# Spectral mixing and expert lookup in one pass: the spectral branch from split half precision to float32, its 16-point stages in 32-row blocks, and a new order of the work

## The chip, the cores and the metric

The kernel runs on one core of a Trainium2 chip. A core has a matrix engine (PE, with its weight loads shown apart as PEld), a vector engine (DVE), a scalar engine (ACT), a general engine (POOL) and a queue for transfers (SP); they share an on-chip memory (SBUF) and a smaller one of eight banks in which PE's results land (PSUM). The metric is the device time of one execution, the median of the runs.

## The reference

For a matrix x of 2048 tokens by 576 features the result is x plus two branches on its normalized rows. The first is a filter in frequency space; the second picks one of 64 experts for each of 32 heads.

```python
def _A_ref(x, w_r, w_i):                       # spectral branch
    X = jnp.fft.rfft2(x, axes=(-2, -1))
    X = X * (w_r + 1j * w_i)
    return jnp.fft.irfft2(X, s=(S, D), axes=(-2, -1))

def _B_ref(x, w_q, k1, k2, u, v):              # one of 8 x 8 experts per head
    q = jnp.einsum("nd,dhc->nhc", xf, w_q)
    s1 = jnp.einsum("nhd,ed->nhe", q[..., :dk], k1)
    s2 = jnp.einsum("nhd,ed->nhe", q[..., dk:], k2)
    ...                                        # the best of each, e = 8 * i1 + i2; softmax over one is 1
    act = _gelu(jnp.einsum("nd,nhkd->nhk", xf, u[top_e]))
    return jnp.einsum("nhk,nhk,nhkd->nd", g, act, v[top_e])

xn = _layernorm(x, axis=-1)
return x + _A_ref(xn, w_r, w_i) + _B_ref(xn, w_q, k1, k2, u, v)
```

## The kernel before

The 2048-point transform over tokens is split into 128 x 16. Tokens lie in 16 tiles of 128 rows. In what follows a tile t or group g is one of 16.

**Front.** `ln` normalizes each tile. `folds` (L713) forms even and odd parts of a row in two steps: sum and difference of 289 elements (POOL, tile `t` in the trace), then sums of 145 (POOL and DVE) and a difference of 2 x 144 (DVE), into a tile shown as `A`. ACT makes `Rs`, the scaled matrix of the 128-point transform, and replicates the 33 middle columns three times (`yl`). `dft128` (L731) multiplies on PE and puts the result into two arrays that hold all tiles, `AB` (four parts of 128 rows) and `ABL` (the left-over 33 rows): ACT copies a half-precision high half, DVE subtracts it from the result for the low half.

**Keys.** 32 transfers bring the weights `wq` of the second branch, and `fold_part` multiplies them with the differences of the keys (`KP`), four column tiles of 32 side by side.

**Spectral middle, per group.** `d_fwd` (L981) does the transform over features: one matmul for the left-over rows and six for each half, since every product of two split numbers is three products (high by high, high by low, low by high). Its result is split again into a tile `A`. `s_fwd` (L998) is the 16-point stage over pairs of groups, in blocks of 64 x 64 (`s` against `A`). `s_mul` (L1021) multiplies by the filter `Wt`, divided by a scale `wx` that `load_w` (L796) and `w_scale` (L806) find from the largest value of the filter: two products on DVE into `t`, two sums on POOL into `y`, a high half on ACT and a low half on POOL into `yh`, and a replication on ACT into `yl`. `s_inv` (L1043) is the 16-point stage back, in two row tiles of 64, with `yh` and `yl` as what is held in PE and `s` as what is moved. Its result is split into `AB` and `ABL` again.

**Second branch, in the same stretch.** `x_t` (L889) loads and splits the transposed rows, `scores` (L904) multiplies them with `MU`, `route` (L930) and `combine` (L950) find the chosen expert and its weight on DVE.

**Last stage, per tile.** `d_inv` (L1076) does the transform over features back, with an eviction by ACT (`yh<-banks,sc`), a product with the scale on DVE, a difference and two sums on POOL. `fin` (L1105) multiplies with `RT`, adds the experts' part, adds x on DVE and stores.

**What sets the order.** All operations are first collected, and then issued in an order set by the table `RANK` and by a model of when each operand is ready (`forward`, L404). `LIMIT` (L205) bounds how many tiles of each kind PSUM holds at a time. So every instruction has the line L528 in the trace, that of the call in `issue`; which step it belongs to is read from the names of its operands. In order listings a number behind a name tells buffers apart.

## Time and profile before

| | us |
|---|---|
| median of 3 runs (lowest, highest) | 226.85 (226.66, 227.8) |
| profiled execution, span | 226.4 |
| PE busy (share of the span) | 198.3 (88%) |
| PEld busy | 136.1 (60%) |
| DVE busy | 195.3 (86%) |
| ACT busy | 135.2 (60%) |
| POOL busy | 150.8 (67%) |
| transfers | 43.43 MB, mean 192 GB/s |

Busy times are sums over the one profiled execution; a matmul counts from its start to its modelled end, so matmuls in a row overlap in it, and how much PE can do is better read from the distance between starts. A row of groups reads: line, engine, operation, out<-in, partitions x elements, count, then busy time, mean of one in ns, then the idle time of the engine just ahead of them and what ended it. A float32 matmul is shown as two records. The chain that ended last is 48% PE and 34% DVE.

### The profile page before, as it was taken

To read this page: it belongs to the slowest core of one execution; us is meant where nothing else is said; L and a number is where in the kernel's file an instruction comes from. 1 tells how busy PE (TensorE), PEld (TensorE's weight loads), DVE (VectorE), ACT (ScalarE), POOL (GpSimd) and SP (SyncE) were. 2 spreads that over 40 slices of the span, in tenths; PEclk is the share of its full clock that TensorE was granted. 3 is DMA by queue.
4 is the path that set the end of the run, shared out by engine and by line. 5 is a ranking of instruction groups with operands and counts; after the bars stand their busy time and mean duration, and the time that the engine had idled before them with its cause. 6 is when DMAs were issued, how large, how long until landed. Compare 5 with 4: busy or idle time off the path is not lost.

```text
span 226.4 us, 5987 instructions
## 1 busy us (share of the span) xinstructions
PE 198.3 (88%) x2287; PEld 136.1 (60%) x2287; DVE 195.3 (86%) x423; ACT 135.2 (60%) x294; POOL 150.8 (67%) x217
## 2 busy tenths in 40 slices
PE   0197959999997999899888999999899999999984
PEld 0185536877675367584464665645566767788762
DVE  1979899997769789763999999999999999999843
ACT  2388877888397797949577577545483332242420
POOL 3889887842097829418668585459794977586880
PEclk9999999999999699999999999999999999999999
DMA  6999999979999995533334322200200002223234
GB/s 209 413 430 410 406 409 408 409 254 380 377 385 402 321 356 141 174 99 107 100 114 153 94 80 61 69 4 0 62 3 0 0 3 104 106 110 154 104 115 148
DMA packets 14572, 43.43 MB, mean 192 GB/s; under 512 B 1872, under 2 KB 4688, under 8 KB 14160
## 3 DMA queue, kind: packets, MB, share of 16 engines
q1 hardware_dynamic: 14544, 43.05, 52.0%
q8 instruction: 18, 0.29, 0.6%
q14 instruction: 10, 0.08, 0.1%
HBM read 38.33 MB, written 4.72 MB: 190 GB/s over the span
## 4 chain that ended last, share of the span: by engine, by line
PE 48%; DVE 34%; issue 7%; POOL 4%; ACT 4%; DMA 2%; DVEq 0%; ACTq 0%; POOLq 0%
PE banks L528 48%; DVE MT L528 8%; DVE w L528 6%; DVE t L528 6%; DVE XN L528 3%; POOL t L528 2%; DVE mx L528 2%; DVE A L528 2%; DVE AB L528 2%; DMA XN<-in_x_dram 2%; DVE st L528 1%; POOL A L528 1%; DVE ABL L528 1%; DVE rr L528 1%; ACT yh L528 1%
## 5 line engine op out<-in xcount | busy, mean ns | idle before, releaser
L528 PE MATMUL banks<-MU,xT 128*128 128x512 f16 x192 | 47.5, 379 | 1.1 <-DVE t L528 0.9
L528 POOL TENSOR_TENSOR xT<-xf,xT 128x512 f16<-128x512 f32 (+1 forms) x32 | 26.2, 819 | 16.6 <-ACT xT L528 14.2
L528 POOL TENSOR_TENSOR y<-t,t 128x289 f32<-128x289 f32 x32 | 22.6, 727 | 20.6 <-DVE t L528 20.3
L528 PE MATMUL banks<-c,AB 128*128 128x145 f16 (+1 forms) x384 | 35.2, 227 | 0.0
L528 POOL TENSOR_TENSOR A<-t 128x145 f32<-128x145 f32 (+2 forms) x48 | 31.2, 665 | 5.3 <-DVE t L528 3.1
L528 PEld LDWEIGHTS <-AB 128*128 128x128 f16 x384 | 32.2, 121 | 3.5 <-issue 1.4
L528 PEld LDWEIGHTS <-xT 128*128 128x128 f16 x224 | 20.6, 99 | 22.2 <-issue 2.1
L528 POOL TENSOR_TENSOR t<-XN 128x289 f32<-128x289 f32 x32 | 24.0, 770 | 8.8 <-DVE A L528 4.1
L528 ACT ACTIVATE yh<-banks,sc 128x580 f32<-128x580 f32 x16 | 11.9, 744 | 23.8 <-PE banks L528 16.9
L528 POOL TENSOR_TENSOR yh<-y,yh 128x578 f16<-128x578 f32 x16 | 21.9, 1377 | 5.4 <-ACT yh L528 4.5
L528 DVE SCALAR_TENSOR_TENSOR t<-banks,wx,Wt 128x578 f32<-128x578 f32 x32 | 24.1, 807 | 0.5 <-PE banks L528 0.4
L528 PE MATMUL banks<-A,c 128*128 128x288 f32 x64 | 21.8, 422 | 1.5 <-POOL A L528 0.9
L528 PE MATMUL banks<-Rs,yl 128*99 128x128 f32 x64 | 11.2, 305 | 13.5 <-ACT Rs L528 13.4
L528 PE MATMUL banks<-w,KP 128*32 128x288 f32 x256 | 22.0, 441 | 0.8 <-DVE mm__94 L528 0.8
L528 DVE TENSOR_TENSOR AB<-banks,AB 128x512 f16<-128x512 f32 x32 | 21.4, 675 | 1.3 <-ACT AB L528 0.7
L528 PE MATMUL banks<-c,ABL 99*128 99x289 f16 (+1 forms) x64 | 18.6, 291 | 1.4 <-DVE t L528 1.0
L528 ACT ACTIVATE AB<-banks 128x512 f16<-128x512 f32 x32 | 18.6, 587 | 2.0 <-PE banks L528 1.9
L528 PE MATMUL banks<-Rs,A 128*128 128x128 f32 x128 | 19.0, 298 | 0.0
L528 PEld LDWEIGHTS banks<-Rs,A 128*128 128x128 f32 x128 | 17.1, 209 | 2.5 <-issue 1.4
L528 PEld LDWEIGHTS banks<-Rs,yl 128*99 128x99 f32 x64 | 8.3, 180 | 16.6 <-ACT Rs L528 15.5
L528 DVE TENSOR_REDUCE MT<-w 128x128 bf16<-128x896 bf16 (+1 forms) x16 | 18.1, 1139 | 0.0
L528 ACT ACTIVATE ABL<-banks 99x256 f16<-99x256 f32 x32 | 12.0, 379 | 9.7 <-PE banks L528 9.6
(124 smaller groups left out, 433.3 us busy)
## 6 DMA issues: line engine op xcount, KB each, us to landing
w<-in_wq_dram SPq DMA_DIRECT2D x32, 576.0 KB, 7.0
xf<-in_xT_dram SPq DMA_DIRECT2D x16, 320.0 KB, 3.7
Wt<-in_W_dram SPq DMA_DIRECT2D x8, 578.0 KB, 6.1
out_dram<-XN SPq DMA_DIRECT2D x14, 288.0 KB, 2.1
XN<-in_x_dram SPq DMA_DIRECT2D x3, 1154.0 KB, 10.6
s<-in_s_dram SPq DMA_DIRECT2D x16, 192.0 KB, 3.4
XN<-in_x_dram SPq DMA_DIRECT2D x2, 577.0 KB, 4.6
c<-in_c_dram SPq DMA_DIRECT2D x1, 868.5 KB, 9.8
```

The costliest lines, as they stand in the source:

```text
L528: fn(*[x.place() if isinstance(x, _Ps) else x for x in args], **{k: x.place() if isinstance(x, _Ps) else x for k, x in kw.items()})
```

## The change

The filter's scale and all splits of the spectral branch go; `AB`, `ABL` and the constants are float32. Every product of split numbers becomes one float32 matmul, every split eviction one copy. The scale that was left goes into `RT`. `d_fwd` and `d_inv` work on two tiles at once, with the left-over rows in four row tiles of 32 (`ABL`, four accumulators in four banks). `s_fwd` works on four groups at once in 16 blocks of 32 x 32, real and imaginary part one after the other. `s_inv` has four row tiles of 32 (`y` held, `iv` moved, 64 columns). `dft128` puts its left-over rows into four column tiles of 32. In `route` a reduction over seven becomes three maxima in half the width. The transfers of `s16` (3.07 MB) become `fw` and `iv` (1.57 MB). A string `PICK` says for each of some 370 simple operations which engine does it (v DVE, a ACT, g POOL), and `RANK` is new. Lines that longer functions lose stand in the kernel above.

```diff
@@ -18,12 +18,6 @@
...
-    s16 = np.concatenate(_hl(fw * 64) + _hl(iv), 2)
...
+    fw = fw.reshape(4, 4, 128, 96).transpose(0, 2, 1, 3).astype(np.float32)
+    iv = iv.reshape(8, 2, 128, 96).transpose(0, 2, 1, 3).astype(np.float32)
...
+PICK = (
+    "vgvgagvvvvaavggvgaavggvvaagggvaavgvvvaaavgvgvaavgvvavavvvgvavvggvvaavggvvvavvvvaavgvvvavagvvvgavgggv"
...
 RANK = (
-    2, 13, 11, 15, 48, 86, 12, 14, 6, 4, 3, 5, 1, 53, 51, 54, 58, 7, 0, 8, 10, 9, 18, 21, 24, 20, 16, 23, 29,
...
+    256, 294, 356, 417, 432, 525, 87, 484, 865, 888, 985, 269, 467, 374, 627, 757, 101, 541, 404, 387, 622,
...
-LIMIT = {"x": 2, "a": 4, "b": 4, "c": 4, "s": 2, "f": 1, "m": 2}
+LIMIT = {"x": 2, "a": 4, "b": 4, "q": 8, "c": 4, "s": 2, "f": 1, "m": 2}
...
+class _Flex:
...
+    def _of(self, calls):
...
+        c = PICK[n] if n < len(PICK) else self.pick
+        eng, m, args, kw = calls[c]
+        getattr(plan.of[c], m)(*args, **kw)
...
+    def tt(self, out, a, b, op):
...
+    def copy(self, out, x, scale=None):
...
-    AB = K([128, 2, 4, S], F16, "AB")
-    ABL = K([128, 2, S], F16, "ABL")
+    AB = K([128, 4, S], F32, "AB")
+    ABL = K([128, S], F32, "ABL")
...
     def folds(t):
         xn = XN[:, t]
...
+        e = T([128, 2, L], F32, "eo", 4, "t1")
+        FG.tt(e[:, 1], xn[:, 0:289], xn[:, 576:287:-1], OP.subtract)
+        FV.tt(e[:, 0], xn[:, 0:289], xn[:, 576:287:-1], OP.add)
+        F = T([128, 2, L], F32, "F", 6, "A2")
+        FV.tt(F[:, 1, 0:145], e[:, 1, 0:145], e[:, 1, 288:143:-1], OP.add)
         V.scalar_tensor_tensor(F[:, 0, 0:145], e[:, 0, 0:145], rr[:, 2, t:t + 1], e[:, 0, 288:143:-1],
                                op0=OP.add, op1=OP.add)
...
+        FV.tt(F[:, :, 145:289], e[:, :, 143::-1], e[:, :, 145:289], OP.subtract)
+        Rs = T([128, 128], F32, "Rs", 4, "act")
+        FA.copy(Rs, Rm, rr[:, 0, t:t + 1])
+        FF[t] = (F, Rs)
     @staged
     def dft128(t):
-        F, FL, Rs = FF.pop(t)
+        F, Rs = FF.pop(t)
         p = PS("x")
-        m = p[:, 0].rearrange("p (h e) -> p h e", e=4)
-        l = p[:99, 1, 0:256].rearrange("p (h e) -> p h e", e=4)
+        m = p[:, 0].rearrange("p (h e) -> p h e", e=2)
+        l = p[:, 1, 0:128].rearrange("p (h e) -> p h e", e=2)
         for c in range(4):
             b, s = divmod(c, 2)
             o = 161 if s else 0
             P.matmul(p[:, 0, 128 * c:128 * c + 128], F[:, b, o:o + 128], Rs, start=True, stop=True)
...
+        for c in range(4):
+            b, s = divmod(c, 2)
+            o = 145 if s else 128
+            P.matmul(p[32 * c:32 * c + 32, 1, 0:128], F[:, b, o:o + 32], Rs, start=True, stop=True,
+                     tile_position=(0, 32 * c))
+        FP.copy(AB.rearrange("p c (h n) -> p (c h) n", n=32)[:, :, 2 * t:2 * t + 2], m)
+        FP.copy(ABL.rearrange("p (h n) -> p h n", n=32)[:, :, 2 * t:2 * t + 2], l)
...
+        V.tensor_scalar(RT, RT, sc[:, 10:11], 4.0 / 1179648.0 / 4096.0, op0=OP.mult, op1=OP.mult)
...
-        A.activation(j, w, AF.Abs, accum_out=wm[:, g // 2:g // 2 + 1])
...
-        V.tensor_reduce(v0, wv, axis=AX, op=OP.max)
+        V.tensor_tensor(wv[:, :, 192:384], wv[:, :, 0:192], wv[:, :, 192:384], op=OP.max)
+        V.tensor_tensor(wv[:, :, 320:448], wv[:, :, 192:320], wv[:, :, 320:448], op=OP.max)
+        V.tensor_tensor(v0.rearrange("p (t m) -> p t m", t=2), wv[:, :, 320:384], wv[:, :, 384:448], op=OP.max)
...
     def d_fwd(g):
-        p = PS("a")
+        ps = [PS("a"), PS("a")]
+        plan.pack = {p.tile for p in ps}
+        pv = [p[:, :, 0:290].rearrange("p c (q l) -> p c q l", q=2) for p in ps]
+        for q in range(2):
+            n = slice(128 * (g + q), 128 * (g + q) + 128)
+            for b in range(2):
+                for c in range(2):
+                    P.matmul(pv[b][:, c, q, :], AB[:, 2 * b + (c ^ b), n], dc[:, b, c, :], start=(q == 0), stop=False)
+        for q in range(2):
+            n = slice(128 * (g + q), 128 * (g + q) + 128)
+            for c in range(2):
+                for b in range(2):
+                    i = 2 * b + (c ^ b)
+                    r = slice(32 * i, 32 * i + 17 - i % 2)
+                    P.matmul(pv[b][:, c, q, :], ABL[r, n], dl[r, :], start=False, stop=(q == 1), tile_position=(32 * i, 0))
+        plan.pack = set()
+        t = T([128, 2, 2, 2, 145], F32, "A2", 6)
         for b in range(2):
-            P.matmul(p[:, b, :L], ABLg[:99, b, g, :], dl[:99, b, :], start=True, stop=False)
+            FP.copy(t[:, :, b].rearrange("p q c l -> p c q l"), pv[b])
+        for q in range(2):
+            A2[g + q] = t[:, q].rearrange("p b c l -> p b (c l)")[:, :, :L]
+    PF = {}
+    @staged
+    def s_fwd(g, m):
+        ps = [PS("q", (128, 512)) for q in range(4)]
+        plan.pack, plan.cap = {p.tile for p in ps}, 1000
+        for b in range(2):
+            w = 32 * (0, 1, 1, 2)[2 * m + b]
+            for k in range(4):
+                r = slice(32 * k, 32 * k + 32)
+                for q in range(4):
+                    o = 32 * (k ^ q)
+                    P.matmul(ps[q][o:o + 32, :L], FW[g][r, q, w:w + 32], A2[g + q][r, b, :], start=(b == 0), stop=(b == 1),
+                             tile_position=(32 * k, o))
+        plan.pack, plan.cap = set(), 900
+        for q in range(4):
+            PF[g + q] = ps[q]
+    @staged
+    def s_mul(g, m):
+        x, w = PF.pop(g)[:, :L].unsqueeze(1).to_broadcast([128, 2, L]), Wt[g]
+        if m == 0:
+            Y[g] = T([128, 2, L], F32, "y", 6)
+            V.tensor_tensor(Y[g], x, w, op=OP.mult)
+            return
+        y, t = Y[g], T([128, 2, L], F32, "t1", 4)
+        V.tensor_tensor(t, x, w, op=OP.mult)
+        FG.tt(y[:, 0], y[:, 0], t[:, 1], OP.subtract)
+        FG.tt(y[:, 1], y[:, 1], t[:, 0], OP.add)
+    @staged
+    def s_inv(g):
+        p, s = PS("c", (128, 4, 2, 4, 64)), IV[g]
+        for q in range(NQ):
+            y = Y.pop(g + q)
+            for c in range(3):
+                for ri in range(2):
+                    for k in range(4):
+                        r = slice(32 * k, 32 * k + 32)
+                        o = (0, 161, 49)[c]
+                        P.matmul(p[:, k, q, c, :], y[r, ri, o:o + 128], s[r, q, 32 * ri:32 * ri + 64],
+                                 start=(ri == 0), stop=(ri == 1), tile_position=(32 * k, 0))
+        for q in range(NQ):
+            pq = p[:, :, q]
+            FP.copy(ABg[:, :, g + q, :].rearrange("p c (k n) -> p c k n", k=4),
+                    pq[:, :, 0:2].rearrange("p k c (b n) -> p (c b) k n", b=2))
+            for b in range(2):
+                FP.copy(ABLg[64 * b:64 * b + 64, g + q, :].rearrange("p (k n) -> p k n", k=4),
+                        pq[64:128, :, 2, 32 * b:32 * b + 32])
+    def d_inv(t):
+        ps = [PS("a"), PS("a")]
+        plan.pack = {p.tile for p in ps}
+        pv = [p[:, :, 0:290].rearrange("p c (q l) -> p c q l", q=2) for p in ps]
+        for q in range(2):
+            for b in range(2):
+                for c in range(2):
+                    P.matmul(pv[b][:, c, q, :], ABt[:, 2 * (c ^ b) + b, :, t + q], ic[:, b, c ^ b, :], start=(q == 0), stop=False)
+        for q in range(2):
             for c in range(2):
...
+                for b in range(2):
+                    i = 2 * b + (c ^ b)
+                    r = slice(32 * i, 32 * i + 32)
+                    P.matmul(pv[b][:, c, q, :], ABLt[r, :, t + q], il[r, :], start=False, stop=(q == 1),
+                             tile_position=(32 * i, 0))
         plan.pack = set()
+        es = T([128, 2, 2, 2, 145], F32, "es", 6, "y")
+        eo = T([128, 2, 2, L], F32, "eo2", 4, "t1")
+        y = T([128, 2, D], F32, "yy", 6, "A2")
+        for b in range(2):
+            FP.copy(es[:, b].rearrange("p c q l -> p c (q l)"), ps[b][:, :, 0:290])
+            V.tensor_tensor(eo[:, b, :, 0:145], pv[b][:, 0], es[:, b, 1], op=OP.add)
+            FG.tt(eo[:, b, :, 288:144:-1], es[:, b, 0, :, 0:144], es[:, b, 1, :, 0:144], OP.subtract)
         for q in range(2):
...
+            FG.tt(y[:, q, 0:289], eo[:, 0, q], eo[:, 1, q], OP.add)
+            FG.tt(y[:, q, 575:288:-1], eo[:, 0, q, 1:288], eo[:, 1, q, 1:288], OP.subtract)
         return y
...
-    for r in range(3):
+    for r in range(2):
         x_t(r)
...
+    for g in range(0, 16, 4):
+        for q in (g, g + 2):
+            d_fwd(q)
+            if q > 2:
+                load_w(q)
+            load_iv(q)
+        if g:
+            load_fw(g)
+        for m in range(2):
+            s_fwd(g, m)
+            for q in range(4):
+                s_mul(g + q, m)
+        for q in (g, g + 2):
+            s_inv(q)
+            r = q // 2
+            scores(r)
+            if r < 6:
+                x_t(r + 2)
             route(r)
...
             combine(r)
...
+    y = d_inv(0)
+    for t in range(0, 16, 2):
+        n = d_inv(t + 2) if t < 14 else None
+        for q in range(2):
+            fin(t + q, y[:, q])
+        y = n
...
```

PE, around the first return of the 16-point stage. Before (`c_72` the constants, `yh_136` the split products, `s_0_114` the stage's matrix):

```order
L528 LDWEIGHTS AB
L528 MATMUL banks<-c_72,AB 128x144
L528 LDWEIGHTS AB
L528 MATMUL banks<-c_72,AB 128x145
...
L528 LDWEIGHTS yh_136
L528 MATMUL banks<-s_0_114,yh_136 128x128
```

and now, with the loads of the weights inside the float32 matmuls (`A_93` the evicted columns):

```order
L552 MATMUL banks<-c_72,AB 128x145 x8
L552 MATMUL banks<-c_72,ABL 128x145 x8
L552 MATMUL banks<-w,KP 32x288 x8
L552 MATMUL banks<-A_93,fw 32x289 x32
L552 MATMUL banks<-w,KP 32x288 x4
L552 MATMUL banks<-A_93,fw 32x289 x32
L552 MATMUL banks<-w,KP 32x288 x8
L552 MATMUL banks<-c_72,AB 128x145 x8
L552 MATMUL banks<-c_72,ABL 128x145 x8
L552 MATMUL banks<-w,KP 32x288 x8
L552 MATMUL banks<-iv,y 128x64 x96
```

Four groups go through the forward stage in two sets of 32 blocks, and four come back in one run of 96; groups of the wq fold stand between.

DVE, at the end of the front. Before:

```order
L528 TENSOR_TENSOR AB<-banks,AB 128x128x4
L528 TENSOR_TENSOR ABL<-banks,ABL 33x64x4
L528 TENSOR_TENSOR AB<-banks,AB 128x128x4
L528 SCALAR_TENSOR_TENSOR A_0_98<-t_0_96,rr 128x145
L528 TENSOR_TENSOR A_0_98<-t_0_96 128x2x144
```

and now:

```order
L552 TENSOR_TENSOR A_93<-t_92 128x145
L552 CAST id_98<-c_68 128x128
L552 TENSOR_TENSOR t_92<-XN 128x289 x2
L552 SCALAR_TENSOR_TENSOR A_93<-t_92,rr 128x145
L552 TENSOR_TENSOR A_93<-t_92 128x2x144
L552 COPY AB<-banks 128x256x2
L552 TENSOR_TENSOR t_92<-XN 128x289
L552 COPY ABL<-banks 128x64x2
```

The subtractions for low halves are gone from DVE, and sums of 289 and 145 elements that were POOL's have come to it.

POOL, from the products with the filter to what `s_inv` needs. Before:

```order
L528 TENSOR_TENSOR y_134<-t_0_96,t_0_106 128x289
L528 TENSOR_TENSOR y_134<-t_0_106,t_0_96 128x289
L528 TENSOR_TENSOR y_135<-t_1_97,t_1_107 128x289
L528 TENSOR_TENSOR y_135<-t_1_107,t_1_97 128x289
L528 TENSOR_TENSOR yh_136<-y_134,yh_136 128x578
```

and now:

```order
L552 TENSOR_TENSOR y<-y,t_92 128x289 x4
L552 TENSOR_SCALAR xf<-xf,bx 128x640
L552 TENSOR_TENSOR y<-y,t_92 128x289 x2
L552 COPY xT<-MT 128x128
L552 TENSOR_TENSOR xT<-xf,xT 64x128
L552 TENSOR_TENSOR y<-y,t_92 128x289 x6
```

The sums stand alone; no subtraction for a low half follows them.

More of the change, by code (lines that the diff above doesn't have):

```diff
@@ L335, in cost, with port_of @@
         return 66 + n / 0.96 / r + (60 if m == "scalar_tensor_tensor" and ptr else 0), 145.0
+    def port_of(self, eng, m, out, ins):
+        sb = [x for x in ins if x.space != PSUM and int(np.prod(x.shape[1:])) > 1]
+        return eng == "gpsimd" and len(ins) > 0 or eng == "vector" and out.space != PSUM and (
+            len(sb) > 1 or m in ("tensor_copy", "tensor_scalar") and len(sb) == 1 == len(ins))
     def add(self, eng, fn, m, args, kw):
@@ L342, in add @@
         c, lat = self.cost(eng, m, out, ins, kw)
-        sb = [x for x in ins if x.space != PSUM and int(np.prod(x.shape[1:])) > 1]
-        port = eng == "gpsimd" and len(ins) > 0 or eng == "vector" and out.space != PSUM and (
-            len(sb) > 1 or m in ("tensor_copy", "tensor_scalar") and len(sb) == 1 == len(ins))
+        port = self.port_of(eng, m, out, ins)
         sh = _parts(ins[0]) if eng == "tensor" else None
@@ L349, in add @@
         if (eng == "tensor" and last is not None and last.eng == eng and last.stage == self.stage
-                and last.cost + c < 900 and (last.tiles == tiles or last.tiles | tiles <= self.pack)):
+                and last.cost + c < self.cap and (last.tiles == tiles or last.tiles | tiles <= self.pack)):
             op, i = last, len(self.ops) - 1
@@ L981, in d_fwd @@
     def d_fwd(g):
-        p = PS("a")
-        for b in range(2):
-            P.matmul(p[:, b, :L], ABLg[:99, b, g, :], dl[:99, b, :], start=True, stop=False)
-            for c in range(2):
-                cs = slice(0, 145) if b == c else slice(145, 289)
-                for n, (ha, hb) in enumerate(((0, 0), (0, 1), (1, 0))):
-                    P.matmul(p[:, b, cs], ABg[:, ha, 2 * b + c, g, :], dc[:, b, hb, cs], start=False,
-                             stop=(c == 1 and n == 2))
-        t = T([128, 2, 2, L], F16, "A2", 2)
```

347 lines of the change are left out of this document (107 added, 240 removed), and 118 rows, old and new, of the table RANK.

## The prediction

> **What bounds the kernel now.** I read the busy time by stage first. The cuts are the first matmul of the spectral branch (53), the first score matmul (94.3), the first inverse column matmul of the last stage (171.4) and the last output matmul (223). The columns are the window, its length, then busy time and count for PE, weight loads, DVE, ACT and POOL, then granted clock, DMA share and GB/s.
>
> ```profile
> 0.00:53.00 53.00, 38.00 (x335) 28.52 (x336) 44.74 (x134) 37.32 (x103) 37.58 (x73) 1.00 0.95 372
> 53.00:94.30 41.30, 38.09 (x633) 26.49 (x629) 33.60 (x77) 33.19 (x65) 24.35 (x29) 0.96 0.90 325
> 94.30:171.40 77.10, 73.37 (x938) 43.58 (x935) 70.14 (x132) 49.35 (x100) 51.20 (x61) 1.00 0.25 72
> 171.40:223.00 51.60, 48.85 (x390) 37.50 (x390) 46.28 (x84) 15.36 (x29) 37.69 (x55) 1.00 0.22 84
> ```
>
> After 53 PE is busy 92 to 95% of every stage, with DVE close behind. Before 53 it is not PE: 38.0 of 53. The waits of PE after 53 (us in total, times, longest) name what PE lacks:
>
> ```profile
> PE banks L528 <- DVE t L528: 4.0, 6, 1.3
> PE banks L528 <- ACT yl L528: 1.0, 1, 1.0
> PE banks L528 <- POOL A L528: 0.9, 1, 0.9
> PE banks L528 <- DVE A L528: 0.8, 1, 0.8
> ...
> PE banks L528 <- DVE AB L528: 0.4, 2, 0.2
> ...
> PE banks L528 <- DVE ABL L528: 0.2, 1, 0.2
> ```
>
> So two questions decide: what the new matmuls cost PE, and what the shorter chains of evictions give back. A busy PE includes matmuls spaced out by others, so I cost matmuls by the distance between starts, not by their durations.
>
> **Rates of the old matmuls.** PE's timeline at a few places (start, busy, then the group):
>
> ```profile
> 84.87 0.85 PE L528 MATMUL banks<-s,yh 64*128 64x128 f16 x24 [0.28 <-DVE t L528]
> 85.53 0.51 PE L528 MATMUL banks<-s,yl 64*99 64x128 f16 x12
> 85.87 0.85 PE L528 MATMUL banks<-s,yh 64*128 64x128 f16 x24
> ...
> 89.35 0.30 PE L528 MATMUL banks<-c,ABL 99*128 99x289 f16 x1
> 89.48 0.55 PE L528 MATMUL banks<-c,AB 128*128 128x145 f16 x6
> 89.87 0.29 PE L528 MATMUL banks<-c,ABL 99*128 99x289 f16 x1
> ...
> 94.31 1.90 PE L528 MATMUL banks<-MU,xT 128*128 128x512 f16 x8
> 96.14 0.84 PE L528 MATMUL banks<-s,yh 64*128 64x128 f16 x24
> ...
> 97.25 1.68 PE L528 MATMUL banks<-A,s 64*64 64x289 f16 x48
> 98.86 0.60 PE L528 MATMUL banks<-MU,xT 128*128 128x512 f16 x2
> ```
>
> The forward and inverse column transforms (d_fwd, d_inv) take 89.87 − 89.35 = 0.52 per half tile, so 1.04 per tile and 33.3 for 32 tiles. The 16-point stage forward (s_fwd) takes 1.61 per pair of groups with the change of tile shape (0.1) in it: 1.5 × 8 = 12.0. Backward (s_inv) it takes 85.87 − 84.87 = 1.00 per group, 16.0 in all; 24 matmuls in 0.66, two row tiles at a time, are 0.055 per pair. Scores take (96.14 − 94.31 − 0.12)/8 = 0.213 per matmul.
>
> **Rates for the new ones.** The rows that show float32:
>
> ```profile
> 191.71 0.65 PE L528 MATMUL banks<-A,c 128*128 128x288 f32 x2
> 192.19 0.41 PE L528 MATMUL banks<-vS,MT 128*128 128x288 f16 x2
> 192.44 0.41 PE L528 MATMUL banks<-A,c 128*128 128x288 f32 x1
> ...
> 64.53 1.18 PE L528 MATMUL banks<-w,KP 128*32 128x288 f32 x16
> 65.64 0.43 PE L528 MATMUL banks<-Wt,on 128*128 128x64 f32 x2
> ...
> 63.49 0.97 PEld L528 LDWEIGHTS banks<-Wt,on 128*128 128x128 f32 x8
> ...
> L528 PEld LDWEIGHTS banks<-Wt,on 128*128 128x128 f32 x10 | 1.3, 190 | 0.5 <-issue 0.5
> ```
>
> A float32 matmul is two records. One of 288 columns takes 192.19 − 191.71 = 0.48, so 0.24 per record; of 145 columns it is an estimate of 0.242 for both. The wq fold runs four column tiles side by side: 16 records (two groups of four) take 1.11 up to the next shape, of which I put 0.12 down to the change of shape, so 0.49 per group: four small tiles cost what one full matmul does. Weight loads of full float32 tiles, with matmuls of only 64 columns between them: eight in 0.97, less the last one's own 0.19, over seven, are 0.111 apart.
>
> *d_fwd and d_inv.* Per pair of tiles 8 full matmuls of 145 columns and 8 of the left-over rows, in two groups of four row tiles: 16 × (8 + 2) × 0.242 = 38.7, so **+5.4**. The bounds: all four row tiles side by side as the wq fold's column tiles are (my value), or each alone, 16 × (8 + 8) × 0.242 = 62. I take the first because two row tiles already run side by side in s_inv: an fp16 matmul of 288 columns takes (192.44 − 192.19)/2 = 0.125, so one of 128 columns 0.055, and a pair of row tiles takes no more.
>
> *s_fwd.* Per four groups and per half (real, imaginary) 32 blocks of 32 × 32, in two sets of 16: 4 × 2 × 2 × 0.48 = 7.7, so **−4.3**. The old blocks of 64 × 64 are 48 in 1.5, or 0.125 for four at once, which is one fp16 pass of 289 columns; four column tiles do not lose either. Sixteen at once are in no row: at half that overlap it would be 15.4.
>
> *s_inv.* Per two groups 48 matmuls of 64 columns, in 12 sets of four row tiles, two records each: 8 × 12 × 2 = 192 passes. The stationary operand is new for every one (32 rows × 128 columns). If a pass goes at the old rate of a pair, 0.053, this is 10.2; if the four loads go side by side, at the 0.111 of one full float32 load, 21.3; if two at a time, 42.6; one after another, 85. The loads of `Wt,on` are the nearest row (float32, 128 columns, 64 columns moved), so I take 21.3, **+5.3**. The Trainium skill, "TensorE: Matmul & The Clock Gate", section "Weight-path perf modes — Fast Weight Load (FWL) and DoubleRow", says that the fast load of weights is not taken for FP32. The trace agrees: the loads of `Wt,on` are 0.11 apart, while six fp16 matmuls with their loads take 0.39. By the rule alone the loads would hold the passes as in my value.
>
> Three groups of the wq fold now stand behind the first spectral matmul (3 × 0.49 = +1.5), six small float32 products for the filter scale go with a change of shape each (6 × 0.34 = −2.0), and there are about three changes of shape more (+0.3). In all PE's work after the first spectral matmul rises by 6.2: **+6**. Before, it was 156.9: 33.3 + 12.0 + 16.0 from above, scores 224 × 0.213 = 47.7, outputs 32 × (0.48 + 0.25) = 23.4, 124 records of the wq fold 15.0, and 9.5 for transposes, scales and changes of shape.
>
> **The front, up to the first spectral matmul.** Its groups, by engine:
>
> ```profile
> L528 POOL TENSOR_TENSOR t<-XN 128x289 f32<-128x289 f32 x32 | 24.0, 770 | 8.8 <-DVE A L528 4.1 <-DMA XN<-in_x_dram 3.2 <-POOL mv L528 0.7
> L528 POOL TENSOR_TENSOR A<-t 128x145 f32<-128x145 f32 x16 | 8.4, 530 | 0.9 <-PE banks L528 0.2 <-ACT yl L528 0.2
> ...
> L528 DVE TENSOR_TENSOR AB<-banks,AB 128x512 f16<-128x512 f32 x16 | 10.6, 675 | 0.9 <-ACT AB L528 0.7
> L528 DVE TENSOR_TENSOR A<-t 128x288 f32<-128x288 f32 x16 | 7.3, 462 | 0.7 <-POOL t L528 0.7
> L528 DVE SCALAR_TENSOR_TENSOR A<-t,rr 128x145 f32<-128x145 f32 x16 | 7.1, 455 | 0.0
> L528 DVE TENSOR_TENSOR ABL<-banks,ABL 33x256 f16<-33x256 f32 x16 | 6.4, 406 | 1.6 <-ACT ABL L528 1.6
> ```
>
> Operations of DVE that read two operands from SBUF do not run beside POOL's. This is seen later in the program, on the same multiply, alone and beside POOL:
>
> ```profile
> 151.40 0.61 DVE L528 TENSOR_TENSOR w<-w,wt 128x896 bf16<-128x896 bf16 x1
> ...
> 154.68 1.70 DVE L528 TENSOR_TENSOR w<-w,wt 128x896 bf16<-128x896 bf16 x1
> ...
> 153.27 2.62 POOL L528 TENSOR_TENSOR yh<-y,yh 128x578 f16<-128x578 f32 x2
> ```
>
> POOL ends at 155.89, and the DVE operation that started at 154.68 ends 0.5 later, at its usual length behind it. So the folds of the front are one queue for both engines: 24.0 + 8.4 + 7.3 + 7.1 = 46.8 of its 53. The change moves 17 of the 32 sums and differences of 289 elements to DVE, and 9 of the 16 of 145; four of the 16 wide folds go the other way. On POOL that is 15 × 0.77 + 7 × 0.53 + 4 × 0.77 = 18.3; on DVE 17 × 0.46 + 12 × 0.46 + 9 × 0.30 + 7.1 = 23.1 (0.30 is an estimate from the 0.462 of 288 elements; at 0.455 it is 24.5). The queue falls to 41.4, **−5**, if DVE has room: its 17.0 of subtractions for low halves go, 8.7 of folds come, and 8 of the 32 copies come to it at no more than 0.675. The rest of the copies are on ACT, which loses the 16 replications. The bounds are 0 (something else is next, such as the loads or the normalization) and −8 (the 41.4 with no gap, behind the 3.2 in which POOL waits for rows). The first spectral matmul then starts at 48.
>
> **The stalls.** From 53.0 to 223 are 170.0; demand by the rates above is 156.9, so 13 are lost: the waits quoted, the clock of 0.96 over 41.3 us (1.7), and many small ones. On removed chains hang DVE t 4.0 (products with the filter scale), ACT yl 1.0, POOL A 0.9, DVE A 0.8 and AB with ABL 0.6, together 7.3. What these chains were, in whole-program rows:
>
> ```profile
> L528 POOL TENSOR_TENSOR y<-t,t 128x289 f32<-128x289 f32 x32 | 22.6, 727 | 20.6 <-DVE t L528 20.3
> L528 POOL TENSOR_TENSOR yh<-y,yh 128x578 f16<-128x578 f32 x16 | 21.9, 1377 | 5.4 <-ACT yh L528 4.5 <-PE banks L528 0.7
> ...
> L528 ACT ACTIVATE AB<-banks 128x512 f16<-128x512 f32 x32 | 18.6, 587 | 2.0 <-PE banks L528 1.9
> ```
>
> Per group the path from s_mul to s_inv was two POOL sums (1.45), an ACT copy (0.68), a POOL subtraction (1.38) and an ACT replication (0.53); now it is two sums. Each return to AB was an ACT copy (0.587) and a DVE subtraction (0.675); now it is one copy. I take the 7.3 and the 1.7 of the clock as gained, **−9**; 4 stay. The bounds are 0 and −13. It is no gain in DVE's load: about 90 us of its work go (subtractions, scaled products, one of the two long reductions) and about 88 come (products of 578 elements at an estimated 0.75, folds, copies), so DVE stays near 193. If its cover goes, each microsecond of DVE costs one, since it stands at 91 to 98% of stretches after 110. POOL falls from 151 to about 100 and ACT from 135 to about 72.
>
> **Sum.** 226.4 − 5 + 6 − 9 = **218 us**. It is made against the profiled execution, 226.4; the median of the runs, 226.85, is 0.2% above it, less than what a measurement tells apart.
>
> **Rivals.**
>
> *B, loads of row tiles are cheap.* In s_inv each tile loads only 32 rows; if four go side by side at the pace of the old pairs, it takes 10.2 instead of 21.3, and the time is **207**. For it: the old s_inv loads new weights for each matmul and holds 0.055 per pair. Against it: those are fp16, and the one float32 row with short matmuls has 0.11.
>
> *C, the stalls stay.* s_fwd, d_fwd and s_inv now each take four of PSUM's eight banks at a time, so two of them fill it, and the eight products of s_mul stand in a row on DVE: 8 × 0.75 = 6 us in which the next set must wait for banks. If the stalls stay but for the 1.7 of the clock: 226.4 − 5 + 6 − 1.7 = **226**. For it: DVE is as full as before. Against it: 7.3 of the 13 hang on chains that go.
>
> *D, slower: the 32-row tiles overlap less than fully.* One mechanism: PE starts the tiles of a set one behind the other, so that a set lasts longer than one full matmul. The rows bound it between 1 time and 4 or 16 times; I price it at 1.3 for four row tiles and 1.5 for sixteen. The left-over rows (7.7) cost +2.3, s_fwd (7.7) +3.9, s_inv (21.3) +6.4, in all 12.6: **231**. It decides from +9 on, that is from 1.24 for all three (36.7 × 0.24). Against it: the rows of the wq fold and of the 64 × 64 blocks lose nothing. The Trainium skill, "TensorE: Matmul & The Clock Gate", section "Part 3: Packing small matmuls — row/col tiling", gives a measured gain of 3.07 for four row tiles and 10.6 for sixteen tiles of 32 × 32. By it the two factors would be 1.30 and 1.51, an estimate; no row here has four row tiles or sixteen blocks.
>
> *E, slower: row tiles load one after another.* Two at a time, s_inv takes 42.6 and the left-over rows 6 more: **245**; all four in series, 302. It decides as soon as a pass takes 0.155 instead of 0.111. Against it: two row tiles of s_inv at 0.055 a pair.
>
> That the change does not do what it says is part of C: the listing shows the split products gone, so only a new wait could keep their time.
>
> **Numbers.** A (218) 0.46, B (207) 0.24, C (226) 0.15, D (231) 0.09, E (245 and up) 0.06. The range is 205 to 229: B at its lower end with the better front, C at its upper; what is left out is D and E. A measurement of this kernel tells 0.5% (1.1 us) from no change. Faster: A 0.45, B 0.24, C 0.06, so 0.75. Same: 0.01 of A and 0.07 of C, 0.08. Slower: 0.02, 0.09 and 0.06, so 0.17. Faster cases alone reach from 204 to 223.
>
> **What would show it.** In the new profile: the first spectral matmul at 48 (step one; at 53 the shared queue was not the bound). A group of s_inv's 48 matmuls from start to next at 2.7 us (1.3 is B, 5.3 or more is E); 32 blocks of s_fwd at 0.96; a pair of d_fwd at 2.42. PE's waits after the first spectral matmul at 4 in total (over 10 is C), with DVE's products or the banks named. DVE busy near 193 and POOL near 100. The prediction is wrong in kind if PE's demand, not its waits, moved by more than 10 either way.

## The result: slower, and the profile after

The changed kernel takes 254.04 us (median; lowest 252.48, highest 255.19) beside 227.3 for the kernel before (four runs, three of which are those of the first table): a ratio of 1.1176, with a 95% interval of 1.1122 to 1.123. The forecast was 218, with a range of 205 to 229. The profiled execution of the changed kernel has a span of 252.3, so 25.9 are to be found beside 226.4. The ratios below leave out runs over 1.5% above the fastest of their kernel, one each of `e4_both`, `e5_oldfolds` and `e10_contig_reorder` and three of the four of `e9_half_reorder`, which the medians hold.

The stages of the changed kernel, cut as before at the first spectral matmul (53.7), the first score matmul (115.1), the first matmul of `d_inv` (175.7) and the last output matmul (249). The columns are those of the first table of the prediction.

```profile
53.70:115.10 61.40, 56.72 (x1047) 42.43 (x1045) 37.70 (x83) 19.82 (x42) 19.40 (x22) 0.94 0.70 245
115.10:175.70 60.60, 59.53 (x855) 33.55 (x852) 53.56 (x105) 19.59 (x42) 30.40 (x39) 1.00 0.23 63
175.70:249.00 73.30, 73.30 (x447) 57.93 (x446) 61.30 (x132) 11.53 (x22) 31.16 (x42) 1.00 0.17 63
```

The first spectral matmul starts 0.7 later than before, and the tail behind the last output matmul is as long as it was (3.3 against 3.4). So nearly all of the loss, 195.3 against 170.0, lies between. The last stage alone grew from 51.6 to 73.3, and in it PE has no idle time at all. The stage ahead of the first score grew by 20.1 and the one behind it fell by 16.5, as work moved from one to the other (see e6). PE's waits over the whole program (us in total, times, longest):

```profile
PE banks L552 <- DVE act L552: 10.5, 1, 10.5
PE banks L552 <- DVE A L552: 8.5, 3, 7.1
PE banks L552 <- issue: 2.0, 1, 2.0
...
PE banks L552 <- DVE t L552: 0.7, 1, 0.7
...
```

The first two belong to the front. After 53.7 only 5.9 are left (0.7 of `DVE A`, 2.0 of issue, 0.7 of `DVE t`, and 2.5 of three smaller rows). So the waits did shrink, and PE's own work grew. PE's timeline shows where, by the distance between starts:

```profile
116.09 1.61 PE L552 MATMUL banks<-A,fw 32*32 32x289 f32 x64
117.63 1.90 PE L552 MATMUL banks<-MU,xT 128*128 128x512 f16 x8
...
123.60 2.15 PE L552 MATMUL banks<-c,AB 128*128 128x145 f32 x16
125.67 0.78 PE L552 MATMUL banks<-c,ABL 17*128 17x145 f32 x16
126.38 0.61 PE L552 MATMUL banks<-MU,xT 128*128 128x512 f16 x2
...
127.35 2.91 PE L552 MATMUL banks<-iv,y 32*128 32x64 f32 x96
130.19 2.76 PE L552 MATMUL banks<-MU,xT 128*128 128x512 f16 x12
...
182.90 3.57 PE L552 MATMUL banks<-c,AB 128*128 128x145 f32 x16
186.39 1.17 PE L552 MATMUL banks<-c,ABL 32*128 32x145 f32 x16
187.50 2.33 PE L552 MATMUL banks<-MU,xT 128*128 128x512 f16 x10
```

| us | predicted | here | times | more than predicted |
|---|---|---|---|---|
| set of `s_fwd` (32 blocks) | 0.96 | 1.54 | 8 | 4.6 |
| pair of `d_fwd` | 2.42 | 2.78 | 8 | 2.9 |
| two groups of `s_inv` | 2.7 | 2.84 | 8 | 1.1 |
| pair of `d_inv` | 2.42 | 4.60 | 8 | 17.4 |

Added up from start to start over the two timelines, waits left out and the clock's losses in, the column transforms (`d_fwd`, `d_inv`) take 62.1 us where they took 34.6, `s_inv` 24.2 (18.5), `s_fwd` 14.1 (13.1), and all else of PE behind the first spectral matmul 88.8 (93.7).

`d_fwd` and `d_inv` issue the same 32 records, but for 16 or 17 rows in the left-over matmuls of `d_fwd` and 32 in those of `d_inv`, which e1 finds equally long; one pair takes 2.78, the other 4.60. What else differs is the operand that PE holds. `d_fwd` reads 128 adjoining columns of `AB`; `d_inv` reads every 16th. The weight loads tell the two apart: in the changed kernel those of `AB` between 175 and 245 (`d_inv`),

```profile
L552 PEld LDWEIGHTS banks<-c,AB 128*128 128x128 f32 x128 | 28.8, 310 | 0.7
```

and between 53 and 97 (`d_fwd`),

```profile
L552 PEld LDWEIGHTS banks<-c,AB 128*128 128x128 f32 x80 | 11.7, 210 | 2.2 <-issue 1.4 <-DVE y L552 0.5
```

The kernel before showed the same step in half precision, in rows that the prediction did not look at (171 to 223, then 53 to 97): 145 ns against 98.

```profile
L528 PEld LDWEIGHTS <-AB 128*128 128x128 f16 x192 | 17.7, 145 | 1.9 <-issue 1.4
...
L528 PEld LDWEIGHTS <-AB 128*128 128x128 f16 x120 | 9.0, 98 | 0.7
```

### The profile page after: what moved, and what is told of

Read it like the earlier page. It is cut to its first block, busy times and chain, and to the rows that moved or that the text cites. A ratio compares the mean times of both kernels' runs of the same rounds, so it can differ in the third digit from the quotient of the medians.

```text
span 252.3 us, 6579 instructions
## 1 busy us (share of the span) xinstructions
PE 225.0 (89%) x2714; PEld 159.1 (63%) x2714; DVE 195.0 (77%) x458; ACT 76.2 (30%) x170; POOL 107.7 (43%) x155
## 4 chain that ended last, share of the span: by engine, by line
PE 72%; DVE 15%; DMA 7%; issue 2%; ACT 1%; SPq 0%; POOL 0%; DVEq 0%; ACTq 0%
PE banks L552 72%; DMA w<-in_wq_dram 6%; DVE y L552 3%; DVE MT L552 2%; DVE w L552 2%; DVE t L552 2%; DMA c<-in_c_dram 2%; DVE A L552 1%; ACT AB L552 1%; DVE ABL L552 1%; DVE xT L552 1%; DVE mx L552 1%; DVE rr L552 0%; DVE xf L552 0%; SPq L552 0%
## 5 line engine op out<-in xcount | busy, mean ns | idle before, releaser
L552 PE MATMUL banks<-c,AB 128*128 128x145 f32 x256 | 50.1, 344 | 0.2 <-DVE ABL L552 0.2
L552 PEld LDWEIGHTS banks<-c,AB 128*128 128x128 f32 x256 | 46.8, 256 | 3.9 <-issue 1.4
L552 PE MATMUL banks<-act,A 128*32 128x128 f32 (+1 forms) x256 | 27.5, 315 | 18.3 <-DVE act L552 10.5
L552 PEld LDWEIGHTS banks<-act,A 128*32 128x32 f32 (+1 forms) x256 | 21.4, 167 | 25.6 <-DVE act L552 10.5
L552 POOL TENSOR_TENSOR y<-y,t 128x289 f32<-128x289 f32 x24 | 18.8, 810 | 30.0 <-DVE t L552 25.7
L552 POOL TENSOR_TENSOR A<-t 128x287 f32<-128x287 f32 (+3 forms) x32 | 23.1, 734 | 15.9 <-DVE t L552 7.3
L552 PEld LDWEIGHTS banks<-iv,y 32*128 32x128 f32 x768 | 23.6, 196 | 5.5 <-issue 2.5
L552 PE MATMUL banks<-iv,y 32*128 32x64 f32 x768 | 24.6, 282 | 2.6 <-issue 2.0
L552 ACT ACTIVATE AB<-banks 128x512 f32<-128x512 f32 x24 | 14.7, 616 | 18.8 <-PE banks L552 17.7
L552 PE MATMUL banks<-c,ABL 32*128 32x145 f32 (+2 forms) x256 | 15.6, 357 | 0.0
L552 DVE TENSOR_TENSOR A<-t 128x288 f32<-128x288 f32 (+3 forms) x32 | 14.6, 467 | 0.2
```

The costliest lines, as they stand in the source:

```text
L552: fn(*[x.place() if isinstance(x, _Ps) else x for x in args], **{k: x.place() if isinstance(x, _Ps) else x for k, x in kw.items()})
```

## The experiments

Theory after the result: the strided float32 loads hold `d_inv` (the 17.4), and sixteen blocks of 32 x 32 overlap less than fully (the 4.6). Rivals: the left-over rows in four row tiles are slow, the front was only ordered badly, or the new order and the engines chosen by `PICK` cost the time. The times (us, median):

| kernel | time | ratio to before (95%) |
|---|---|---|
| changed kernel | 254.04 | 1.1176 (1.1122 to 1.123) |
| `e2_contig` | 244.13 | 1.0695 (1.061 to 1.078) |
| `e3_front` | 251.78 | 1.1069 (1.0987 to 1.1151) |
| `e4_both` | 242.89 | 1.0632 (1.053 to 1.0734) |
| `e5_oldfolds` | 256.59 | 1.1244 (1.1144 to 1.1345) |
| `e6_half` | 241.39 | 1.0595 (1.05 to 1.0689) |
| `e7_before_contig` | 227.85 | 0.9984 (0.9944 to 1.0023) |
| `e8_reorder` | 272.44 | 1.198 (1.1911 to 1.2049) |
| `e9_half_reorder` | 282.92 | none |
| `e10_contig_reorder` | 269.2 | 1.1815 (1.1755 to 1.1875) |

### e1: the rates by themselves

A program of matmuls alone, one form after another, nothing waiting for anything:

```diff
+for s in (1, 2, 4, 8, 16):
+    full(X, 145, s)          # float32, weights are every s-th column, 145 columns moved
+for s in (1, 16, 32):
+    full(H, 145, s)          # the same in half precision
+full(X, 64, 1)
...
+full(X, 288, 1, 24)
...
+rows(X, 32, 64)              # four row tiles of 32
+rows(X, 32, 145)
+rows(X, 17, 145)
+rows(X, 32, 145, 16)
...
+blocks(X, 32, 289)           # sixteen blocks of 32 x 32
```

> This kernel leaves out the whole computation: PE alone runs rows of independent matmuls of the shapes that matter, with nothing beside it. Theory W (a float32 weight load whose columns lie 64 bytes apart in SBUF is slow, and this is what makes the last stage long): records of 145 columns take about 0.13 us with columns side by side and about 0.22 with every 16th column, with half precision at every 16th column unchanged near 0.06. Rival S (the last stage is slow for something around it, such as traffic of other engines or the banks): the stride makes no difference, 0.13 for all. For the small tiles: if PE itself is the reason, a set of four row tiles of 32 rows and 145 columns takes 0.17 to 0.18 a pass, a set of 16 blocks of 289 columns 0.36, and four row tiles with 64 columns 0.11; if the kernel around it is, 0.12, 0.24 and 0.11.

PE's timeline of it. Between the groups stands a marker of one column; a group's length is the marker's start less its own.

```profile
48.39 12.09 PE L36 MATMUL banks<-X 128*128 128x145 f32 x96
60.31 0.28 PE L31 MATMUL banks<-X 128*128 128x1 f32 x2
60.45 12.09 PE L36 MATMUL banks<-X 128*128 128x145 f32 x96
72.38 0.28 PE L31 MATMUL banks<-X 128*128 128x1 f32 x2
72.52 22.66 PE L36 MATMUL banks<-X 128*128 128x145 f32 x96
95.01 0.28 PE L31 MATMUL banks<-X 128*128 128x1 f32 x2
...
118.42 21.30 PE L36 MATMUL banks<-X 128*128 128x145 f32 x96
139.55 0.28 PE L31 MATMUL banks<-X 128*128 128x1 f32 x2
139.69 3.20 PE L36 MATMUL banks<-H 128*128 128x145 f16 x48
142.73 0.33 PE L31 MATMUL banks<-X 128*128 128x1 f32 x2
142.92 3.23 PE L36 MATMUL banks<-H 128*128 128x145 f16 x48
145.98 0.33 PE L31 MATMUL banks<-X 128*128 128x1 f32 x2
...
171.31 11.89 PE L36 MATMUL banks<-X 128*128 128x288 f32 x48
183.04 0.28 PE L31 MATMUL banks<-X 128*128 128x1 f32 x2
...
195.09 6.20 PE L45 MATMUL banks<-X 32*128 32x145 f32 x192
201.22 0.38 PE L31 MATMUL banks<-X 128*128 128x1 f32 x2
...
238.39 7.25 PE L62 MATMUL banks<-X 32*32 32x289 f32 x327
246.13 1.54 PE L62 MATMUL banks<-X 32*32 32x289 f32 x57 [0.49 <-issue]
247.60 0.38 PE L31 MATMUL banks<-X 128*128 128x1 f32 x2
```

A float32 record takes (60.31 − 48.39)/96 = 0.124 with adjoining weights, the same with every second column (8 bytes apart), 0.234 with every fourth (16 bytes) and 0.220 with every 16th. In half precision every 16th column costs nothing: 0.063 and 0.064 per matmul. The Trainium skill, "SBUF — State Buffer", section "Door 1: The DMA port swizzle (why `[64,N]` ≈ `[32,N]`)", says that SBUF is read in lines of 16 bytes and needs at least two accesses in each for its full rate. The float32 rows agree (8 bytes are free, 16 are not); for half precision at 32 bytes the matmuls here show no loss, though the mean load grows from 100 ns to 144.

Four row tiles of 32 rows take 6.13/48 = 0.128 per set of four, against 0.124 for one full record: 1.03, so the left-over rows are no cause; with 17 rows in each tile the set takes the same 0.128. Sixteen blocks take (247.60 − 238.39 − 0.49)/24 = 0.363 per set, against (183.04 − 171.31)/48 = 0.244 for a full record of 288: 1.49. That is the 1.5 by which rival D priced `s_fwd`. The Trainium skill, "TensorE: Matmul & The Clock Gate", section "Measured speedup vs the span model", gives a gain of 10.6 for sixteen blocks, and 16/1.49 = 10.7 agrees; its 3.07 for four row tiles, measured with 512 columns, does not: the rows here, with 145, give 4/1.03 = 3.9. Both gains take a small tile alone to cost as much as a full record, which no run here shows. Of the two expectations for small tiles, the second came true for four row tiles and the first for sixteen blocks.

### e2: contiguous weights in d_inv

```diff
-P.matmul(pv[b][:, c, q, :], ABt[:, 2 * (c ^ b) + b, :, t + q], ic[:, b, c ^ b, :], ...)
+P.matmul(pv[b][:, c, q, :], ABg[:, 2 * (c ^ b) + b, t + q, :], ic[:, b, c ^ b, :], ...)
-P.matmul(pv[b][:, c, q, :], ABLt[r, :, t + q], il[r, :], ...)
+P.matmul(pv[b][:, c, q, :], ABLg[r, t + q, :], il[r, :], ...)
```

All copies into `AB` and `ABL` are waited for as before.

> The changed kernel, in which the inverse column transform reads 128 columns side by side in place of every 16th. It computes with the wrong tokens (this part of the computation is left wrong), but issues the same instructions in the same order, and its first one waits for the same evictions. Theory W: a pair of tiles goes from 4.65 to about 2.95 us, 8 x 1.7 = 13.6 less for PE in the last stage, of which DVE (61 of 73 us busy there) lets about 11 to 13 through: 240. Rival S: 252, no change. Rival R (float32 itself, whatever the stride, makes the stage long): 250 to 252.

PE's timeline:

```profile
177.27 2.14 PE L552 MATMUL banks<-c,AB 128*128 128x145 f32 x16
179.34 0.78 PE L552 MATMUL banks<-c,ABL 32*128 32x145 f32 x16
180.05 1.25 PE L552 MATMUL banks<-MU,xT 128*128 128x512 f16 x5
```

This pair takes 2.78, as one of `d_fwd` does, and eight such pairs would be 14.6 less. Added up from start to start, waits left out, the eight take 23.3 instead of 37.4: 14.1 less, so the stride is nearly the whole difference. The time falls by 9.9, less than the 11 to 13 expected. The last stage shows what keeps the rest:

```profile
175.70:240.00 64.30, 60.68 (x453) 43.41 (x451) 62.77 (x135) 13.16 (x27) 32.85 (x42) 1.00 0.19 70
```

DVE is busy for 62.8 of 64.3: it is next behind PE. PE begins the stage 1.6 later than in the changed kernel and waits 3.5 in it, 3.1 of that for DVE, where it waited for nothing.

### e7: the same in the kernel before

```diff
-P.matmul(p[:, b, cs], ABt[:, ha, 2 * c + b, :, t], ic[:, b, hb, cs], start=False, ...)
+P.matmul(p[:, b, cs], ABg[:, ha, 2 * c + b, t, :], ic[:, b, hb, cs], start=False, ...)
```

> The kernel before, in its own order, with its inverse column transform reading 128 half-precision columns side by side in place of every 16th (wrong tokens in this part). Theory W (only float32 loads of separate columns are slow; in half precision they hide behind the matmuls): 0.52 per half tile as before, 226 to 228, no change. Rival: the kernel before paid for it too, and gains 3 us or more.

No change: 0.9984 (0.9944 to 1.0023). So the stride was free as long as the numbers were of half precision, though each load was longer (145 ns, in e7 97), and it became a price with float32.

### e3 and e5: the front

In e3, POOL's small product for the means of tiles 2 and 3 and what follows from it are issued earlier; in e5 the folds stand on the engines of before, in the new order.

```diff
+for i, j in ((56, None), (59, None), (60, None), (61, None), (75, None), (65, 75), (77, None), (66, 77), (67, 64)):
+    k = order.index(i)
+    d = max(order.index(m) for m in ops[i].deps | ({j} if j else set())) + 1
+    if d < k: order.insert(d, order.pop(k))
```

> The changed kernel with the same instructions, but POOL's small product for the means of tiles 2 and 3, and what DVE and POOL do with it, moved ahead of the sums and statistics of later tiles. Theory Q (one small operation behind others in POOL's queue makes PE wait 7 us, and the granted clock is at half for 5 us after): PE goes on at 16 to 17 in place of 22, at full clock, the first spectral matmul comes at 46 to 48, and the time falls by 5 to 7, to 246. Rival P (the front is bound by PE's own work or the loads): the first spectral matmul stays at 52 to 54 and the time at 252.

In the timeline of the changed kernel PE starts its second run of matmuls at 22,

```profile
22.01 5.26 PE L552 MATMUL banks<-act,A 128*32 128x128 f32 x32 [7.14 <-DVE A L552]
```

and in that of e3, its first runs:

```profile
10.42 4.75 PE L559 MATMUL banks<-act,A 128*32 128x128 f32 x32 [10.42 <-DVE act L559]
16.37 2.96 PE L559 MATMUL banks<-act,A 128*32 128x128 f32 x32 [1.21 <-DVE A L559]
...
24.28 2.37 PE L559 MATMUL banks<-act,A 128*32 128x128 f32 x16 [3.52 <-ACT act L559]
```

The wait of 7.14 goes, PE starts again at 16.37, and a wait of 3.52 for the scaled matrix of a later tile takes part of it back. The first spectral matmul comes at 51.95, not at the 46 to 48 of theory Q. The median falls by 2.3, which the two intervals do not tell apart from nothing. Both edits together (e4) have a ratio of 1.0632 beside the 1.0695 of e2, and these intervals overlap too; the 233 to 236 of two savings that add did not come.

> Both edits together, with the same wrong tokens in the last stage. Theories W and Q: the two savings are in different stages, both bound by PE, and add: 233 to 236. If only W holds, 240; if only Q, 246.

```diff
+for o in ops:                # e5, shortened: sums and differences of 289 and 145 elements on the engines of before
+    if o.flex and 2 <= o.stage <= 38 and ...: c = "v" if len(out.shape) == 3 else "g"; o.calls = [...]
```

> The changed kernel in its own order, but with the folds of the front on the engines of before: both sums of 289 elements and the one of 145 on POOL, the wide difference on DVE. Theory P (from about 30 us on the front is bound by PE's own work, so the shared queue of DVE and POOL was not the bound that the prediction took it for): the first spectral matmul at 53 to 55, the time within 1.5 us of the changed kernel. Rival F (the queue was the bound, and the change of engines is worth its 5 us): the first spectral matmul at 58 or later and 4 to 6 us more.

256.59, with the first spectral matmul at 56.65: three later than in the changed kernel. The two intervals overlap, so by the time alone the folds are not told from no change; by the start of the first spectral matmul their new places give some three of the five us of the forecast, in a front that lost as much elsewhere.

### e6: the new order with half-precision coefficients

`AB`, `ABL` and the constants in half precision, one product each, with the low halves left out:

```diff
-AB = K([128, 4, S], F32, "AB")
-ABL = K([128, S], F32, "ABL")
+AB = K([128, 4, S], F16, "AB")
+ABL = K([128, S], F16, "ABL")
-c16 = K([128, 580 + 145 + 580 + 145], F32, "c16")
+c16 = K([128, 580 + 145 + 580 + 145], F16, "c16")
```

> The changed kernel in its own order, with AB, ABL and the constants of the column transforms in half precision, one product each: the low halves are left out of the computation. Evictions, DVE, ACT and POOL stay as they are; only the float32 price of these transforms on PE goes: a pair falls to about 0.8 us from 2.8 forward and 4.65 backward, 46 us in all. Theory V (DVE is next, with 54 of 61 us busy in the middle and 61 of 73 in the last stage): 53.7 + 52 + 57 + 62 + 3, about 225 to 230, so that the rest of the change (shorter chains, the new order) is worth nothing against the kernel before. Rival G (the rest of the change is a clear gain, only float32 on PE hides it): 206 to 218. Rival H (the new order itself loses): over 235.

241.39, as rival H has it: with the column transforms far below their price in the kernel before, this is still 6% slower. So price alone does not explain the loss. From the first score on, in two windows:

```profile
53.70:115.00 61.30, 50.99 (x945) 33.66 (x945) 37.26 (x83) 19.87 (x43) 19.06 (x21) 0.83 0.71 257
115.00:175.00 60.00, 58.15 (x849) 32.13 (x847) 54.79 (x106) 19.83 (x43) 31.02 (x39) 1.00 0.23 68
175.00:238.00 63.00, 49.14 (x310) 30.25 (x302) 61.71 (x132) 11.05 (x22) 32.16 (x41) 0.92 0.18 69
```

DVE has 54.8 + 61.7 = 116.5 to do behind 115, and 123 us for it. The kernel before had the same 116.4 (70.14 + 46.28) behind its first score, but that came at 94.3. Between the first spectral matmul and the first score, DVE now idles for 24.0 of 61.3 (before: 7.7 of 41.3). The granted clock there is 0.83, so a relieved PE is also a slower one. Taken off the length of the windows, as the prediction did it, the clock is up to 15.5 us (0.17 of 61.3 and 0.08 of 63; 1.7 before), and PE's waits from the first spectral matmul on are 25.9 instead of 9.7. The longest of them in sum is

```profile
PE banks L552 <- DVE t L552: 6.2, 5, 3.5
```

Against the kernel before, e6 thus has some 16 more of waits and up to 14 more of clock, less some 17 of PE's work. No run tells the waits and the clock apart. And in that stretch the new order does more of PE's spectral work. PE's groups by form, of the changed kernel (53.7 to 115.1) and of the kernel before (53 to 94.3):

```profile
L552 PE MATMUL banks<-iv,y 32*128 32x64 f32 x384 | 13.0, 292 | 2.6 <-issue 2.0 <-DVE A L552 0.7
L552 PE MATMUL banks<-c,ABL 17*128 17x145 f32 x56 | 5.4, 308 | 0.0
```

```profile
L528 PE MATMUL banks<-s,yh 64*128 64x128 f16 x120 | 4.2, 216 | 1.6 <-DVE t L528 1.6
L528 PE MATMUL banks<-c,ABL 99*128 99x289 f16 x20 | 5.9, 294 | 0.0
```

Now half of `s_inv` (384 of 768) and seven eighths of `d_fwd` (56 of 64) stand ahead of the first score; before, five of 16 groups (120 of 384) and five eighths (20 of 32). While PE is full everywhere, as it is in the changed kernel, this need cost nothing by itself. Once PE is relieved, as in e6, DVE's late start would be the next bound. The rows fit that, but it is not shown, as no run brought the first score earlier.

### e8, e9 and e10: other orders

The table of ranks of the changed kernel, of e6 and of e2 is replaced by one searched with the rates of e1 (`RANK = (256, 294, 356, ...)` by other numbers, nothing else).

> The changed kernel with another order of the same instructions (another table of ranks, found by a search in which a strided float32 record costs 0.222 us and a record of sixteen blocks 0.363, as the rates measured alone gave them). Nothing else differs. Theory O (the order on record put the second branch 21 us later, and DVE's 116 us behind the first score came late with it): the first score matmul comes before 105, and the time falls to 238 to 246. Theory P (the price of PE's instructions is the whole loss): PE is busy for 189.6 of the 195.3 us between the first spectral matmul and the last output, so an order can save only what lies ahead of that matmul and the 5.7 that are left, and the time stays at 249 to 254.

> The kernel with contiguous float32 weights in the inverse column transform (its tokens are wrong, as the columns are not the right ones), now with an order searched for its own prices; with the order of the change it took 244.1. PE's demand is 15 us below that of the change. Theory O: 228 to 237, between the new order with the strided loads and the kernel before. Theory P: 241 to 244, no more than the front gives.

272.44 and 269.2: both slower than with the order of the change (254.04 and 244.13), against either theory. In e8's timeline the first score stands at 114.85, as late as ever, and in e10's at 121.04, so the aim was missed. The searched orders fitted the model that they were searched with and not the chip: in e8 PE's busy time is 234.7 instead of 225.0, and new waits for DVE stand in it (4.8 for `DVE y` alone). They show only that these two orders are worse.

> The kernel with half-precision coefficients and transforms in one product (low halves left out, so its tokens are rounded more coarsely), now with an order searched for its own prices; with the order of the change it took 241.4. PE has some 46 us less to do in the column transforms. Theory O: the 14 us that it still lost to the kernel before were the order; it falls to 227 or below. Theory X (something else in the change costs, such as DVE's or POOL's operations, which no order mends): it stays at 236 or above.

e9 took 282.92, and even its shortest run, 277.45, is far above the 241.39 of e6. PE is idle for 46.5 us in it, the granted clock is 0.817, and the first score comes at 139.77, so this order too is worse, against either theory. Whether an order exists that starts the second branch early and gives back the loss of e6 stays open. Of the engines that `PICK` chose, only those of the front's folds were put back (e5). No version of the changed kernel here beats the kernel before.

## Why the prediction was wrong, step by step

**The term that failed: d_fwd and d_inv.** The prediction gave both one rate, 0.242 per two records, "all four row tiles side by side", and its bounds were spent on the left-over rows. Those were right (1.03 by e1). What it missed is that `d_inv` holds every 16th column: 0.22 per record instead of 0.124. Of the 17.4 us that `d_inv` took above its forecast, the stride is 14 to 15 (e2). It had the doubt at hand: the same loads took 145 ns instead of 98 in the kernel before. There the matmuls hid it (e7), so no wait and no spacing showed it. `d_fwd`, contiguous, came to 2.78 a pair instead of 2.42 (two changes of tile shape and 0.129 per record): 2.9 more.

**s_fwd.** Costed at full overlap of sixteen blocks, −4.3; the blocks lose a factor of 1.49, and the term came to about 0. Here rival D was right, and its 1.5 too, but it was given 0.09 because the blocks of 64 x 64 lose nothing. They are four, not sixteen, and could not speak for sixteen. For four row tiles D was wrong, and its mechanism, tiles that start one behind the other, no run here shows.

**s_inv.** 2.7 forecast, 2.84 measured (0.118 a pass; in e1, alone, 0.115): right, so rivals B (1.3) and E (5.3 or more) fall. E's "all four in series, 302" adds up to 305 from its own terms.

**PE's work in sum.** From 53.7 to 249 are 195.3; less 5.9 of waits and 3.7 of clock (0.06 of 61.4) PE had 185.7 to do, where the forecast had 163.1. The four terms of the table make 26.0 more, against 22.6 found, so the work taken as unchanged was 3.4 dearer in the forecast than on the chip. The `wq` fold is more than that: the prediction put its 124 records at 15.0, but by its own rate, 0.49 for eight, they are 7.6 without the changes of shape. With the three groups more it stands at 16.5 in the sum, and takes 10.8 from start to start.

**The stalls.** "−9; 4 stay": the named waits after the first spectral matmul are 5.9, and those for the removed chains went (`ACT yl`, `POOL A`, and `DVE t` from 4.0 to 0.7). That fits the mechanism, but does not show it: a PE with 23 us more to do than forecast waits less whatever the chains are, and in e6, with the same chains and a lighter PE, the waits are 25.9, with 6.2 for `DVE t`. The clock's 1.7 did not come back; it is 3.7 now. The sign of rival C, over 10 of waits, is not met here, but e6 leaves C open. With PE full, a shorter chain has nothing to give.

**The front.** "First spectral matmul at 48": it came at 53.7. The prediction summed the folds of POOL and DVE over 53 us and took their queue for the bound. The chain of waits of the kernel before, which it did not read there, has this row (start, length, what):

```profile
32.02 34.07 PE banks L528 x393
```

From 32 on PE alone was the chain, so a shorter queue could help only ahead of 32. There the new order lost 7.1 to one small product queued on POOL behind operations that wait for ACT, and e3 shows that the next wait, 3.5, stands close behind it.

**DVE, POOL and ACT.** 195.0, 107.7 and 76.2, for a forecast of 193, 100 and 72: right. The prediction's closing condition, "wrong in kind if PE's demand, not its waits, moved by more than 10 either way", is what happened: 156.9 by its count before, 185.7 now.

**Not in the prediction at all:** the later start of the second branch, from 94.3 to 115.1. In the changed kernel it hides behind PE; in e6 it is a candidate for what is left of the loss, beside the clock.

## What to carry to other kernels

A matmul's price depends on how its held operand lies in memory and on its type together: before a type is widened, look for weight loads that are longer than their neighbours, even where they cost nothing yet. Find the bound of a stretch from the chain of waits within it, not from a queue's sum over a longer one. A rate seen with four tiles is no evidence for sixteen.

## What was not expected of the hardware

Float32 weights 16 to 64 bytes apart take 0.22 to 0.24 us per record of 145 columns instead of 0.124; 8 bytes apart they cost nothing extra. And the idle time of PE in the front is paid twice. In these slices of the changed kernel, whose PE is idle from 14.9 to 22, the granted clock (third from the end) falls to 0.50 some 2 us into the idle time and is still there 4 us after PE has begun again:

```profile
16.00:18.00 2.00, 0.00 (x0) 0.00 (x0) 1.97 (x9) 1.90 (x7) 0.26 (x2) 0.80 0.96 404
18.00:20.00 2.00, 0.00 (x0) 0.00 (x0) 1.99 (x6) 1.97 (x6) 1.75 (x4) 0.50 1.03 426
...
24.00:26.00 2.00, 2.00 (x16) 1.39 (x14) 2.00 (x7) 1.29 (x5) 0.64 (x2) 0.50 0.64 260
```
